# Three unused buffers that shift the split sums of g within SBUF

## The chip, the cores and the metric

The kernel runs on one core of a Trainium2 chip. The metric is the device time of one execution in microseconds (us), lower is better. A core has a matrix engine (PE, with its weight loads shown apart as PEld), a vector engine (DVE), a scalar engine (ACT), GpSimd (POOL), and SyncE (SP), which here only issues transfers. They share an on-chip memory, SBUF, of 128 partitions; an address below is a byte offset that holds in every partition. "Modulo 256" is that offset's remainder.

## The reference

For four batches of 768 tokens and eight heads of 64, a retention layer runs over the tokens, and a feed-forward layer follows:

```python
state = gamma * state + outer(k[t], v[t])      # per head, t = 0..767
x[t]  = q[t] @ state / sqrt(64)                # 3072 tokens x 512
h = x @ w_in                                   # 512 -> 2048
g = h * clip(h + 3, 0, 6) / 6
out = g @ w_out                                # 2048 -> 512
```

All is float32.

## The kernel before

The feed-forward products are made from float32 numbers that are split into a high and a low part (`high` on ACT, line 219; `low` on DVE, line 222), each of a 32-bit matmul type; a product is three matmuls: high by high, high by low, low by high.

**First stage.** The retention, the conversion of the weights, and h run together. h comes in 96 tiles of 128 features by 512 tokens, twelve matmuls each (line 505). ACT (line 512) and DVE (line 516) turn a tile into g, in one of three buffers `g` of 2,048 bytes, and an ACT-issued transfer writes it to the DRAM tensors `gd` (line 539). The order on PE, DVE, ACT and SP is the order of the code here. The first stage ends with the h tiles of the last token unit; from there only PE keeps the order of the code (`order`), while a scheduler sets the order of the other engines by its own estimates of when inputs are ready.

**Second stage.** out = g @ w_out is made in a scheme of seven block products in place of eight (ids 1 to 7). The tokens are taken in three blocks `sb` of 1,024. Each block has four groups, `GROUPS = ((4, 5), (1, 6), (7,), (2, 3))`, and each group goes over four chunks `c` of the features. For a chunk, two transfers bring g back from `gd` into a buffer `gv`; DVE adds or subtracts its halves (lines 136 and 139) into a kept sum `spare` (or in place); then each operand (`gv`, the sum, or both) is split into a buffer `gc` of 8,192 bytes, ACT writing the high half and DVE the low half; and PE makes twelve matmuls of 512 columns from each `gc` (line 782), with the weights `w` standing and `gc` streaming. Results gather in PSUM (`o`), are scaled and combined into `kept_p`, `kept_q`, `kept_v` and `spare` by ACT and DVE (lines 723, 726, 139), and SP stores them to `out` (line 730). The very last product is cut in pieces, and the last store is issued by ACT.

There are 84 operands, and they go round five `gc` buffers: number n takes buffer n modulo 5. Buffers 0 and 1 (tags `gc0`, `gc1`) lie in the pool `late`; buffers 2, 3 and 4 have one pool each, `left["gc0"]`, `left["gc1"]`, `left["gc2"]`:

```python
i = n_gc % 5
pool = late if i < 2 else left[f"gc{i - 2}"]
```

So seventeen operands use each of buffers 0 to 3, and sixteen use buffer 4. The pools `left` stand one behind the other in the order gv0, gv1, gc2, v, p, gc0, gc1, q, on memory that the first stage used for its conversions, for x and for the three `g` buffers. A tile placed there waits for the last users of the bytes it covers.

Every tile that PE reads in this kernel begins at 0 modulo 256. Some smaller constants do not: `mask` lies at 1568 and `cmask` at 2848, both 32 modulo 256.

Of the kernel before, what the change touches and what calls it, by code (L numbers as in the profile page):

```python
# [9 lines left out]
F32 = mybir.dt.float32  # L10
# [10 lines left out]
P = 128  # L21
# [10 lines left out]
def retention_ffn(ctx: ExitStack, tc: tile.TileContext, qkv, w_in, w_out, dvs, dkc, dqc, dmc, tab, out, B, H, S, D):  # L32
# [59 lines left out]
    edge = ctx.enter_context(tc.tile_pool(name="edge", bufs=1, side="right"))  # L92
# [35 lines left out]
    def nm(s):  # L128
        return f"{s}_{next(serial)}"
# [551 lines left out]
    for u, jj in steps[STEADY:]:  # L681
# [8 lines left out]
    left = {  # L690
        n: ctx.enter_context(tc.tile_pool(name=f"left_{n}", bufs=1, reuse_waits="tile"))
        for n in ("gv0", "gv1", "gc2", "v", "p", "gc0", "gc1", "q")
    }
    ends = ctx.enter_context(ExitStack())
    ps_o = [
        ends.enter_context(tc.tile_pool(name=f"ps_o{i}", bufs=1, space=PSUM, reuse_waits="tile", side=side))
# [215 lines left out]
```

## Time and profile before

| | |
|---|---|
| Median of 3 runs | 572.21 us (571.96 to 573.33) |
| The profiled execution | 572.05 us |
| Its span, first to last instruction | 570.3 us |
| PE, DVE, ACT busy | 99%, 75%, 44% of the span |
| Second stage on PE | 1,008 matmuls from 338.06 us on |
| Granted PE clock | 1.00 throughout |

Busy time is a share of the span. A PE that is called busy may still be paced by something, so the pace (time from one matmul's start to the next) is read from how many matmuls lie in a stretch. The profile's rows name tiles without their buffer numbers; `gc<-gv` and `gc<-spare` are the two kinds of split, and both halves of both kinds are 1,024 elements per partition.

### The profile page before, as it was taken

To read this page: it belongs to the slowest core of one execution; us is meant where nothing else is said; L and a number is where in the kernel's file an instruction comes from. 1 tells how busy PE (TensorE), PEld (TensorE's weight loads), DVE (VectorE), ACT (ScalarE), POOL (GpSimd) and SP (SyncE) were. 2 spreads that over 40 slices of the span, in tenths; PEclk is the share of its full clock that TensorE was granted. 3 is DMA by queue.
4 is the path that set the end of the run, shared out by engine and by line. 5 is a ranking of instruction groups with operands and counts; after the bars stand their busy time and mean duration, and the time that the engine had idled before them with its cause. 6 is when DMAs were issued, how large, how long until landed. Compare 5 with 4: busy or idle time off the path is not lost.

```text
span 570.3 us, 11862 instructions
## 1 busy us (share of the span) xinstructions
PE 563.5 (99%) x4832; PEld 462.6 (81%) x4832; DVE 429.6 (75%) x594; ACT 249.2 (44%) x388; POOL 44.2 (8%) x50
## 2 busy tenths in 40 slices
PE   8999999999999999999999999999999999999997
PEld 6777888888888888888888888888888888888885
DVE  5879879942777678887737989679776698676881
ACT  4863434532444443444434654444335443344430
POOL 3001110220111111122000000000000000000000
PEclk9999999999999999999999999999999999999999
DMA  8946787762656666667543485565744747636611
GB/s 314 369 140 220 232 278 228 259 227 92 220 206 223 216 223 215 231 231 260 165 161 115 150 292 189 175 226 167 263 165 132 240 162 258 206 115 189 213 75 74
DMA packets 60626, 115.68 MB, mean 203 GB/s; under 512 B 6166, under 2 KB 6934, under 8 KB 60572
## 3 DMA queue, kind: packets, MB, share of 16 engines
q1 hardware_dynamic: 46304, 89.54, 47.8%
q10 hardware_dynamic: 14268, 25.39, 11.7%
q8 instruction: 38, 0.62, 0.5%
q14 instruction: 16, 0.13, 0.1%
HBM read 83.45 MB, written 31.46 MB: 201 GB/s over the span
## 4 chain that ended last, share of the span: by engine, by line
PE 94%; DVE 3%; DMA 1%; ACT 0%; issue 0%; SPq 0%; DVEq 0%
PE h L505 45%; PE o L782 40%; PE uz L458 3%; PE y L458 3%; PE sc L458 2%; DMA early<-in_qkv 1%; DMA st<-in_w_in 1%; DVE we L200 1%; DVE x L222 0%; DVE am L381 0%; DVE w L222 0%; DVE g L516 0%; DVE wb L187 0%; DVE xr L609 0%; DVE wb L195 0%
## 5 line engine op out<-in xcount | busy, mean ns | idle before, releaser
L505 PE MATMUL h<-x,w 128*128 128x512 f32 x1152 | 270.1, 393 | 0.2
L505 PEld LDWEIGHTS h<-x,w 128*128 128x128 f32 x1152 | 213.9, 188 | 46.4 <-DVE w L222 0.6
L782 PE MATMUL o<-gc,w 128*128 128x512 f32 x1008 | 228.6, 389 | 0.0
L782 PEld LDWEIGHTS o<-gc,w 128*128 128x128 f32 x1008 | 189.2, 188 | 39.3
L512 ACT ACTIVATE g<-h,three 128x512 f32<-128x512 f32 x96 | 65.8, 687 | 109.7 <-PE h L505 81.1
L516 DVE SCALAR_TENSOR_TENSOR g<-g,h 128x512 f32<-128x512 f32 x96 | 65.5, 684 | 56.2 <-ACT g L512 56.0
L219 ACT ACTIVATE gc<-gv 128x1024 fp32r<-128x1024 f32 x48 | 50.9, 1060 | 61.0 <-PE o L782 55.2
L222 DVE TENSOR_TENSOR gc<-gv,gc 128x1024 fp32r<-128x1024 f32 x48 | 58.7, 1222 | 22.5 <-ACT gc L219 22.5
L219 ACT ACTIVATE gc<-spare 128x1024 fp32r<-128x1024 f32 x36 | 38.2, 1061 | 50.3 <-PE o L782 43.3
L222 DVE TENSOR_TENSOR gc<-spare,gc 128x1024 fp32r<-128x1024 f32 x36 | 44.0, 1221 | 10.1 <-ACT gc L219 10.0
L192 ACT ACTIVATE we<-we,ebias 128x512 int32<-128x512 int32 x32 | 23.0, 719 | 17.1 <-DVE we L183 16.3
L219 ACT ACTIVATE w<-ww 128x384 fp32r<-128x384 f32 (+2 forms) x34 | 18.6, 552 | 24.9 <-DVE ww L206 20.6
L200 DVE SCALAR_TENSOR_TENSOR we<-st,we 128x512 int32<-128x512 int32 x32 | 23.0, 720 | 2.3 <-ACT we L192 2.2
L195 DVE SCALAR_TENSOR_TENSOR wb<-st,wb 128x512 f32<-128x512 uint32 x32 | 23.0, 720 | 0.7
L347 POOL TENSOR_TENSOR qs<-qt,dq 128x512 f32<-128x512 f32 x16 | 23.0, 1439 | 6.3 <-DMA dq<-in_decays_q 6.3
L206 DVE SCALAR_TENSOR_TENSOR ww<-wb,we 128x512 f32<-128x512 f32 x32 | 22.9, 715 | 0.8
L462 ACT ACTIVATE state<-uz 128x256 f32<-128x256 f32 x39 | 14.8, 379 | 19.5 <-PE y L458 9.7
L222 DVE TENSOR_TENSOR w<-ww,w 128x384 fp32r<-128x384 f32 (+2 forms) x34 | 20.4, 604 | 1.5 <-ACT w L219 1.4
L136 DVE TENSOR_TENSOR spare<-spare,gv 128x1024 f32<-128x1024 f32 x12 | 14.7, 1223 | 6.1 <-DMA gv<-gd 6.0
L343 POOL TENSOR_TENSOR kn<-kn,ccst 128x512 f32<-128x512 f32 x8 | 9.0, 1128 | 120.9 <-DMA kn<-in_qkv 85.0
L458 PE MATMUL y<-qs,state 64*64 64x64 f32 x480 | 18.3, 222 | 0.0
L458 PE MATMUL y<-am,vn 64*64 64x64 f32 x512 | 18.1, 219 | 0.0
(69 smaller groups left out, 417.9 us busy)
## 6 DMA issues: line engine op xcount, KB each, us to landing
gd<-g ACTq DMA_DIRECT2D x96, 256.0 KB, 2.9
gv<-gd SPq DMA_DIRECT2D x48, 512.0 KB, 4.7
gv<-gd SPq DMA_DIRECT2D x48, 256.0 KB, 3.0
st<-in_w_in SPq DMA_DIRECT2D x32, 256.0 KB, 3.9
st<-in_w_out SPq DMA_DIRECT2D x16, 512.0 KB, 5.8
early<-in_qkv SPq DMA_DIRECT2D x28, 256.0 KB, 4.6
kt<-in_qkv SPq DMA_DIRECT2D x16, 256.0 KB, 3.5
qt<-in_qkv SPq DMA_DIRECT2D x16, 256.0 KB, 3.9
```

The source lines that it names most:

```text
L192: nc.scalar.activation(out=t["e"], in_=t["e"], func=AF.Relu, scale=8.0, bias=ebias)
L195: nc.vector.scalar_tensor_tensor(out=t["b"].bitcast(F32), in0=lo.bitcast(U32), scalar=2.0**-32, in1=t["b"], op0=ALU.mult, op1=ALU.add)
L200: nc.vector.scalar_tensor_tensor(out=t["e"], in0=hi, scalar=-2147483648, in1=t["e"], op0=ALU.bitwise_and, op1=ALU.bitwise_or)
L206: nc.vector.scalar_tensor_tensor(out=t["w"], in0=t["b"].bitcast(F32), scalar=2.0**-20, in1=t["e"].bitcast(F32), op0=ALU.mult, op1=ALU.mult)
L219: nc.scalar.activation(out=hi, in_=src, func=AF.Copy)
L222: nc.vector.tensor_tensor(out=lo, in0=src, in1=hi, op=ALU.subtract)
L347: nc.gpsimd.tensor_tensor(out=t["qs"], in0=t["qt"], in1=d, op=ALU.mult)
L458: nc.tensor.matmul(out_, lhs, rhs, start=start, stop=True, skip_group_check=True)
L505: nc.tensor.matmul(h, t[:, o, a], xs[u][b][:, k], start=k + n == 0, stop=(k, n) == (NK - 1, 2), skip_group_check=True)
L512: return g, nc.scalar.activation(out=g, in_=h, func=AF.Relu, bias=three).ins
L516: ins = nc.vector.scalar_tensor_tensor(out=g, in0=g, scalar=6.0, in1=h, op0=ALU.min, op1=ALU.mult)
L782: nc.tensor.matmul(acc[i][h] if last else acc[i][:, h], w2c[j][:, RIGHT[i], x, h], gc[:, y, jj], start=j == 0 and n == 0, stop=j == NFP - ...
```

## The change

```diff
     left = {
         n: ctx.enter_context(tc.tile_pool(name=f"left_{n}", bufs=1, reuse_waits="tile"))
         for n in ("gv0", "gv1", "gc2", "v", "p", "gc0", "gc1", "q")
     }
+    for n, edge in (("gc2", 64), ("gc0", 128), ("gc1", 96)):
+        left[n].tile([P, edge // 4], F32, tag="edge", name=nm("edge"))
```

Three buffers are allocated that no instruction touches. They push what stands behind them upwards:

| Tile | Address before | Address after | After, modulo 256 |
|---|---|---|---|
| gc buffer 4 (`gc2`) | 163840 | 163904 | 64 |
| kept_v | 172032 | 172096 | 64 |
| kept_p | 176128 | 176192 | 64 |
| gc buffer 2 (`gc0`) | 180224 | 180416 | 192 |
| gc buffer 3 (`gc1`) | 188416 | 188704 | 32 |
| kept_q | 196608 | 196896 | 32 |

All of these lay at 0 modulo 256. gc buffers 0 and 1, all `gv`, `spare` and all weights stay where they were. Buffer 3 ended at 196608, where the first of the three `g` buffers begins; now it ends at 196896, so it covers the first 288 bytes of that buffer.

No instruction is added or removed, but the scheduler places some differently at the seam between the stages. The three new buffers take three serial numbers, so a name's last number is three higher after the change: what is gc_4239 before is gc_4242 after. It is the fourth operand, the sum of chunk 1, in buffer 3. gc_4236 (after: gc_4239) is the third operand; gc_4270 and gc_4273 (after: gc_4273 and gc_4276) are the fifth and sixth, from chunk 2.

ACT at the seam, high halves, before:

```order
L219 ACTIVATE gc_4236<-gv_4232 128x1024 [waits DMAHW3_49,DMAHW1_49]
L539 DMA gd_74<-g_4151 128x512 [waits DVE_49]
L219 ACTIVATE gc_4239<-spare_4191 128x1024 [waits DVE_49]
L219 ACTIVATE gc_4270<-gv_4266 128x1024 [waits DMAHW6_49,DMAHW5_49,Activation_49]
L219 ACTIVATE gc_4273<-spare_4192 128x1024 [waits DVE_49,PE_49,Activation_49]
L219 ACTIVATE gc_4304<-gv_4300 128x1024 [waits DMAHW0_49,DMAHW2_49,PE_49,Activation_49]
```

ACT at the same place after:

```order
L219 ACTIVATE gc_4239<-gv_4235 128x1024 [waits DMAHW3_49,DMAHW1_49]
L539 DMA gd_74<-g_4151 128x512 [waits DVE_49]
L219 ACTIVATE gc_4273<-gv_4269 128x1024 [waits DMAHW6_49,DMAHW5_49,Activation_49]
L219 ACTIVATE gc_4276<-spare_4195 128x1024 [waits DVE_49,PE_49,Activation_49]
L219 ACTIVATE gc_4242<-spare_4194 128x1024 [waits DMAHW4_49]
L219 ACTIVATE gc_4307<-gv_4303 128x1024 [waits DMAHW0_49,DMAHW2_49,PE_49,Activation_49]
```

The fourth operand's high half has moved behind the two of chunk 2, and it waits for a transfer: the one that writes out the last g tile of the first `g` buffer (g_4097), which ACT issues right behind the relu of the next h tile.

DVE at the seam, sums and low halves, before:

```order
L139 TENSOR_TENSOR spare_4191<-gv_4232 128x1024 [waits DMAHW3_49,DMAHW1_49]
L222 TENSOR_TENSOR gc_4236<-gv_4232,gc_4236 128x1024 [waits Activation_49]
L139 TENSOR_TENSOR spare_4192<-gv_4266 128x1024 [waits DMAHW6_49,DMAHW5_49,PE_49]
L222 TENSOR_TENSOR gc_4239<-spare_4191,gc_4239 128x1024 [waits Activation_49]
L222 TENSOR_TENSOR gc_4270<-gv_4266,gc_4270 128x1024 [waits Activation_49]
L222 TENSOR_TENSOR gc_4273<-spare_4192,gc_4273 128x1024 [waits Activation_49]
L139 TENSOR_TENSOR spare_4192<-gv_4300 128x1024 [waits DMAHW2_49,DMAHW0_49]
```

and after:

```order
L139 TENSOR_TENSOR spare_4194<-gv_4235 128x1024 [waits DMAHW3_49,DMAHW1_49]
L222 TENSOR_TENSOR gc_4239<-gv_4235,gc_4239 128x1024 [waits Activation_49]
L139 TENSOR_TENSOR spare_4195<-gv_4269 128x1024 [waits DMAHW6_49,DMAHW5_49,PE_49]
L222 TENSOR_TENSOR gc_4273<-gv_4269,gc_4273 128x1024 [waits Activation_49]
L222 TENSOR_TENSOR gc_4276<-spare_4195,gc_4276 128x1024 [waits Activation_49]
L222 TENSOR_TENSOR gc_4242<-spare_4194,gc_4242 128x1024 [waits DMAHW4_49,Activation_49]
L139 TENSOR_TENSOR spare_4195<-gv_4303 128x1024 [waits DMAHW2_49,DMAHW0_49]
```

Here too the fourth operand's low half has moved behind those of the fifth and the sixth.

PE uses the operands in the unchanged order. Around the fourth operand it now reads:

```order
L784 MATMUL o_4199<-gc_4239,w_353_2955 128x512 x3
L784 MATMUL o_4200<-gc_4242,w_312_2629 128x512 [waits Activation_49]
L784 MATMUL o_4200<-gc_4242,w_312_2629 128x512 [waits DVE_49]
L784 MATMUL o_4200<-gc_4242,w_312_2629 128x512
L784 MATMUL o_4200<-gc_4242,w_353_2955 128x512 x3
L784 MATMUL o_4200<-gc_4242,w_312_2629 128x512 x3
L784 MATMUL o_4200<-gc_4242,w_353_2955 128x512 x3
L784 MATMUL o_4199<-gc_4273,w_396_3300 128x512 x3
```

The first matmul of an operand waits for ACT (the high half), the second for DVE (the low half). What moved is which engine step is the last one that PE waits for there; the fifth operand, which had such waits of its own, has none left, since the fourth is now made behind it.

## The prediction

> **What bounds the kernel now.** The first view is the page: its busy shares and its chain of work that ended last.
>
> ```profile
> PE 563.5 (99%) x4832; PEld 462.6 (81%) x4832; DVE 429.6 (75%) x594; ACT 249.2 (44%) x388; POOL 44.2 (8%) x50
> PE 94%; DVE 3%; DMA 1%; ACT 0%; issue 0%; SPq 0%; DVEq 0%
> ```
>
> PE carries 94% of the chain. The chain in order of time (columns: start, length, what) says how its second stage runs, which is the only stage with moved tiles.
>
> ```profile
> 289.03 49.19 PE h L505 x216
> 338.22 228.49 PE o L782 x1008
> 566.73 0.42 DVE kept_v L726
> 567.16 0.33 DVEq L908
> ```
>
> The 1,008 matmuls of the second stage stand on the chain as one unbroken piece: 228.49 us / 1,008 = 226.7 ns each. So nothing that ACT, DVE or a transfer does there reaches the end of the program today, and there are just two ways in which the change can: the pace of a matmul changes, or a first wait appears in this piece.
>
> Is the pace steady? The third view counts work by stretches of the second stage (length, then busy time and count of each engine, the clock, the transfers' share and rate).
>
> ```profile
> 358.00:396.00 38.00, 38.00 (x169) 31.48 (x168) 30.35 (x26) 17.47 (x18) 0.00 (x0) 1.00 0.61 194
> 396.00:434.00 38.00, 38.00 (x170) 31.45 (x169) 29.44 (x26) 14.84 (x15) 0.00 (x0) 1.00 0.58 194
> 434.00:472.00 38.00, 38.00 (x169) 31.47 (x168) 30.24 (x26) 17.59 (x18) 0.00 (x0) 1.00 0.61 194
> 472.00:510.00 38.00, 38.00 (x169) 31.47 (x168) 29.51 (x26) 14.84 (x15) 0.00 (x0) 1.00 0.59 194
> 510.00:548.00 38.00, 38.00 (x170) 31.45 (x169) 29.89 (x26) 17.59 (x18) 0.00 (x0) 1.00 0.52 166
> ```
>
> Every stretch of 38 us has 169 or 170 matmuls, the one or two at its edges counted in, at a clock of 1.00. DVE is busy 29.4 to 30.4 us of it, ACT 14.8 to 17.6. The groups show what the two do with the gc tiles, and the waits who is ahead of whom.
>
> ```profile
> L222 DVE TENSOR_TENSOR gc<-gv,gc 128x1024 fp32r<-128x1024 f32 x48 | 58.7, 1222 | 22.5 <-ACT gc L219 22.5
> L219 ACT ACTIVATE gc<-gv 128x1024 fp32r<-128x1024 f32 x48 | 50.9, 1060 | 61.0 <-PE o L782 55.2 <-DVE gc L222 3.3 <-DMA gv<-gd 2.5
> ...
> ACT gc L219 <- PE o L782: 98.6, 62, 1.7
> ```
>
> ACT stands still 98.6 us in all, in 62 waits, because PE still reads the buffer that ACT wants: the makers of operands are ahead of PE and are throttled by it.
>
> **The change part by part.** *Nothing is computed less or more.* Five gc buffers remain five, so the distance by which the makers may run ahead is the same.
>
> *The pace of PE on moved buffers.* Buffers 2, 3 and 4 hold 17 + 17 + 16 = 50 of 84 operands, so 50 x 12 = 600 of the 1,008 matmuls stream from an address that is no longer 0 modulo 256. No matmul of this trace does that, so the cost is bounded from both sides. Upwards: 512 float32 columns are 2,048 bytes, eight pieces of 256 bytes from an aligned start and nine from another; if the pace went with the pieces, each matmul would cost 226.7 / 8 = 28.3 ns more, 17.0 us in all. Downwards: the quickest 512-column stream of the trace is that of the small bf16 tables.
>
> ```profile
> 6.01 0.82 PE L559 MATMUL t<-bits 6*128 6x512 bf16 x3
> ...
> L559 PE MATMUL t<-bits x6: 371/379/384, 6.0 to 17.2; 6*128 6x512 bf16 x6
> ```
>
> Three of them take 0.82 us, the last one's own 0.379 included, so their pace is (0.82 - 0.379) / 2 = 0.2205 us, 6.2 ns under that of the second stage; 600 x 6.2 = 3.7 us is the most that a better address could give. Between +17.0 and -3.7 us I take zero, by the nearest rows that do read SBUF off 0 modulo 256: DVE's products with `mask` and `cmask` (both 32 modulo 256), beside its product with `early` (0 modulo 256).
>
> ```profile
> L381 DVE TENSOR_TENSOR am<-sc,mask 128x512 f32<-128x512 f32 x12 | 7.9, 684 | 3.8 <-issue 3.6
> L426 DVE TENSOR_TENSOR am<-sc,cmask 128x512 f32<-128x512 f32 x16 | 11.0, 688 | 6.2 <-PE y L458 6.2
> L609 DVE TENSOR_TENSOR xr<-y,early 128x512 f32<-128x512 f32 x8 | 5.5, 686 | 4.3 <-PE y L458 4.3
> ```
>
> 684 and 688 ns off the boundary, 686 ns on it: the address shows no price on DVE. For ACT's and DVE's writes into the moved buffers I take zero as well, by the same rows, and the cover is large. PE uses one operand in 12 x 0.2267 = 2.72 us, so 14 in 38 us, of which 14 x 50 / 84 = 8.3 are moved; DVE has 38 - 30.35 = 7.65 us free in its fullest stretch. Each moved low half could take 7.65 / 8.3 = 0.92 us more than today before PE would wait. A gain there would be worth nothing.
>
> The stores of kept_p, kept_v and kept_q now read from 64 and 32 modulo 256. All but the last are far behind PE. Of that one the row is
>
> ```profile
> out<-kept_v ACTq DMA_DIRECT2D x1, 128.0 KB, 1.7
> ```
>
> and I take no change for it. [...]
>
> *The seam.* The fourth operand is now split behind the fifth and sixth. This is the only place where PE may wait. The time line of DVE and ACT there before (start, length, then the step; DVE: sum and low half of the third and so on, as listed with the change):
>
> ```profile
> 338.06 9.23 PE L782 MATMUL o<-gc,w 128*128 128x512 f32 x40
> ...
> 338.84 1.05 ACT L219 ACTIVATE gc<-gv 128x1024 fp32r<-128x1024 f32 x1
> ...
> 339.58 1.22 DVE L139 TENSOR_TENSOR spare<-gv 128x1024 f32<-128x1024 f32 x1
> ...
> 340.72 1.22 DVE L222 TENSOR_TENSOR gc<-gv,gc 128x1024 fp32r<-128x1024 f32 x1
> 340.84 1.06 ACT L219 ACTIVATE gc<-spare 128x1024 fp32r<-128x1024 f32 x1 [0.94 <-DVE spare L139]
> 341.80 1.04 ACT L219 ACTIVATE gc<-gv 128x1024 fp32r<-128x1024 f32 x1
> 341.85 1.22 DVE L139 TENSOR_TENSOR spare<-gv 128x1024 f32<-128x1024 f32 x1
> ...
> 342.99 1.22 DVE L222 TENSOR_TENSOR gc<-spare,gc 128x1024 fp32r<-128x1024 f32 x1
> 343.19 1.06 ACT L219 ACTIVATE gc<-spare 128x1024 fp32r<-128x1024 f32 x1 [0.34 <-DVE spare L139]
> 344.12 1.22 DVE L222 TENSOR_TENSOR gc<-gv,gc 128x1024 fp32r<-128x1024 f32 x1
> ```
>
> Two habits are read from it: steps of DVE follow each other at 1.135 us (340.72, 341.85, 342.99, 344.12), those of ACT at 0.96 (340.84, 341.80); and a result is used 0.04 to 0.12 us after its end (the sum ending at 340.80, ACT at 340.84; the sum ending at 343.07, ACT at 343.19). PE reaches the fourth operand's second matmul, which needs its low half, at 338.06 + 37 x 0.2267 = 346.45. Before, that half ended at 342.99 + 1.22 = 344.21, 2.2 us early. Now:
>
> - ACT makes the fifth operand's high half behind the third's, long before DVE asks for it at 342.99.
> - The sixth needs the sum of chunk 2, which ends at 343.07: ACT from 343.11 or 343.19, until 344.17 or 344.25. DVE starts its low half 0.04 later, 344.21 to 344.29, a little behind the 344.12 at which it is free.
> - The fourth's high half goes 0.96 behind the sixth's and ends by 345.21, before PE's first use at 346.22. Its low half starts 1.135 us behind the sixth's, 345.35 to 345.42, ends 1.22 later, 346.57 to 346.64, and reaches PE at about 346.61 to 346.68.
>
> PE waits 0.16 to 0.23 us there; I take **0.2 us**, with 0.1 and 0.4 as ends, since a handover can take 0.04 or 0.12 more. Queued behind that wait is all the rest of PE's stage, so it goes to the end in full. The new wait for the transfer costs nothing: ACT issues it at 335.54, and the slowest of the 96 lands in 6.7 us,
>
> ```profile
> 335.54 0.33 ACTq L539 DMA_DIRECT2D gd<-g  x1
> ...
> DMA to landing us min/median/max: 2.0/2.9/6.7
> ```
>
> at 342.24, 1.8 us before ACT comes to that step. What is late next is DVE by some 0.15 us at the low half of the seventh operand (chunk 3), which PE needs only at 338.06 + 73 x 0.2267 = 354.6.
>
> **The sum.** The profiled execution took 572.05 us with a span of 570.3; +0.2 gives a span of 570.5 and 572.25 us. The runs' median is 572.21, 0.16 above that execution, so the forecast for a median is 572.4 us.
>
> **The rivals.**
>
> *PE reads a moved buffer more slowly (slower).* Place: the 600 matmuls; price: up to 28.3 ns each, 589 us; if only a finer piece of 64 bytes counts, buffer 3 alone pays, 17 x 12 = 204 matmuls x 226.7 / 32 = 7.1 ns, 1.4 us, 573.8. It decides from (1.72 - 0.2) / 600 = 2.5 ns a matmul. For it: no matmul of this trace has ever read off the boundary, so nothing excludes it. Against it: the DVE rows above. [...] No run so far shows a matmul that could tell.
>
> *DVE or ACT writes a moved buffer more slowly (slower).* Only past 0.92 us for each low half. Twice today's 1.135 would make 8.3 x 1.135 - 7.65 = 1.8 us of waiting in 38 us, some 10.7 us over the 228 of the stage: 583 us. The even cost in the rows above speaks against it.
>
> *Streams collide today (faster).* All tiles start at the same remainder; if PE lost time to ACT's and DVE's writes at the same position, spreading the buffers would give up to 3.7 us, 568.7 us. Against it: DVE's and ACT's steps drift against PE's (1.135 and 0.96 against 0.2267 us), so their positions meet in every way, yet no stretch is slower than another, and the last of them, with a lighter transfer load of 166 GB/s, is none the faster.
>
> *The seam costs more.* If the transfer landed at 346 rather than 342.2, PE would wait 2 us: 574.4. Its landing is bounded by 96 others, so this is a part of the slow tail.
>
> **How the numbers follow.** A measurement of this kernel tells about 0.3%, 1.7 us, from no change. The forecast, an unchanged pace with 0.2 us at the seam, has 0.71, and its own range is 571.7 to 573.4. A slower PE has 0.12, slower ACT or DVE 0.04, a longer seam 0.03: slower 0.19 together. Collisions that vanish have 0.10. The range goes from 570.4, half-way into the gain, to 576.0, past the finer piece and the longer seam.
>
> **What would show it.** Right: an L782 row of 1,008 matmuls with the same pace in every stretch (169 or 170 in 38 us), and one idle time of PE near 346.4 us, 0.1 to 0.4 us long, ended by DVE's gc step. Wrong: 38-us stretches with fewer than 168 matmuls, or waits of PE on L219 or L222 beyond the seam, or gc steps on ACT or DVE off 1,060 and 1,222 ns. The forecast falls if the pace differs between matmuls from buffers 0 and 1 and the rest.

## The result

| | Before | Changed |
|---|---|---|
| Median | 572.22 us (571.96 to 573.33, 4 runs) | 576.24 us (576.07 to 576.42, 4 runs) |
| Span of the profiled execution | 570.3 us | 574.3 us |

The changed kernel is slower: 1.0067 of the time before, with a 95% interval of 1.0049 to 1.0084. The prediction was wrong: it said 572.4 us and no measurable change, and the measured time lies 0.24 us past the upper end of its range. One of the ten runs of the first experiment below took 1,443 us, and the ratio there is formed without it.

The page after the change looks almost the same. The chain of work in order of time (start, length, what) shows where the 4 us lie; its last pieces are these.

```profile
289.08 49.19 PE h L505 x216
338.27 8.47 PE o L784 x37
346.75 223.95 PE o L784 x971
570.73 0.42 DVE kept_v L728
571.15 0.33 DVEq L910
```

The first stage ends where it ended (338.27 against 338.22), and the 216 h matmuls before it take 49.19 us as before. The one piece of 1,008 matmuls is now two, 37 and 971: that is the forecast wait at the seam. But the 971 behind it take 223.95 us, 230.6 ns each, where 226.7 was forecast. The stretches of 38 us (length, busy time and count of each engine, clock, transfers) say the same:

```profile
358.00:396.00 38.00, 38.00 (x167) 30.89 (x166) 29.46 (x26) 17.43 (x17) 0.00 (x0) 1.00 0.60 193
396.00:434.00 38.00, 38.00 (x167) 30.92 (x166) 29.16 (x26) 14.87 (x14) 0.00 (x0) 1.00 0.58 194
434.00:472.00 38.00, 38.00 (x167) 30.96 (x166) 29.14 (x26) 17.30 (x17) 0.00 (x0) 1.00 0.57 180
472.00:510.00 38.00, 38.00 (x167) 30.99 (x166) 29.60 (x26) 14.26 (x15) 0.00 (x0) 1.00 0.62 209
510.00:548.00 38.00, 38.00 (x167) 30.89 (x166) 29.12 (x25) 17.45 (x17) 0.00 (x0) 1.00 0.52 166
```

167 matmuls in each, where there were 169 or 170, at a clock of 1.00, and PE called busy throughout. A slower pace hides in a "busy" engine: no idle time appears in any of these stretches. The groups (moved and unmoved buffers together) show that ACT and DVE take no longer for their splits, and are still ahead:

```profile
L222 DVE TENSOR_TENSOR gc<-gv,gc 128x1024 fp32r<-128x1024 f32 x48 | 58.6, 1221 | 24.7 <-ACT gc L219 24.6
L219 ACT ACTIVATE gc<-gv 128x1024 fp32r<-128x1024 f32 x48 | 50.9, 1060 | 63.1 <-PE o L784 51.5 <-DVE gc L222 6.8 <-ACT gc L219 2.7
...
ACT gc L219 <- PE o L784: 89.1, 53, 1.8
```

The 1,008 matmuls are used in a known order, twelve to an operand, and operand n lies in buffer n modulo 5. So the starts of the matmuls in the trace can be sorted by buffer: the time from an operand's first matmul to the next operand's first, divided by twelve, averaged over the operands of a buffer (the fourth operand, with the wait at the seam, and the last left out). All paces by buffer below are made in this way.

| gc buffer | 0 | 1 | 2 | 3 | 4 |
|---|---|---|---|---|---|
| before: begins at, modulo 256 | 0 | 0 | 0 | 0 | 0 |
| pace, ns | 226.7 | 226.7 | 226.7 | 226.7 | 226.7 |
| changed: begins at, modulo 256 | 0 | 0 | 192 | 32 | 64 |
| pace, ns | 228.6 | 226.7 | 233.3 | 233.1 | 229.8 |

Each moved buffer has its own pace, the same in the second and the third block of tokens, and within 0.4 ns of that in the first. Buffer 0, which did not move but follows buffer 4, is slow in the first five of its twelve matmuls each time that it does, and then back at 226.7. Over 226.7 this makes 17 x 12 x 6.7 = 1.4 us in buffer 2, 17 x 12 x 6.4 = 1.3 in buffer 3, 16 x 12 x 3.1 = 0.6 in buffer 4, 17 x 12 x 2.0 = 0.4 in buffer 0: 3.7 us together. At the seam two spacings (from one matmul's start to the next) of 399 and 339 ns stand in place of 227: 0.28 us. With the 0.05 us by which the stage begins later these are the 4.0 us of the span.

### The profile page after: what moved, and what is told of

The parts are those of the page before. It is cut to its first block, busy times and chain, and to the rows that moved or that the text cites. A ratio compares the mean times of both kernels' runs of the same rounds, so it can differ in the third digit from the quotient of the medians.

```text
span 574.3 us, 11862 instructions
## 1 busy us (share of the span) xinstructions
PE 567.6 (99%) x4832; PEld 462.6 (81%) x4832; DVE 424.7 (74%) x594; ACT 249.1 (43%) x388; POOL 45.7 (8%) x50
## 4 chain that ended last, share of the span: by engine, by line
PE 95%; DVE 2%; DMA 2%; issue 0%; SPq 0%; ACT 0%; DVEq 0%
PE h L505 47%; PE o L784 40%; PE uz L458 3%; PE y L458 3%; PE sc L458 2%; DMA st<-in_w_in 1%; DMA early<-in_qkv 1%; DVE am L381 0%; DVE x L222 0%; DVE xr L609 0%; DVE we L200 0%; SPq L157 0%; DVE ww L206 0%; ACT w L219 0%; DVE w L222 0%
## 5 line engine op out<-in xcount | busy, mean ns | idle before, releaser
L784 PE MATMUL o<-gc,w 128*128 128x512 f32 x1008 | 232.6, 392 | 0.0
L219 ACT ACTIVATE gc<-gv 128x1024 fp32r<-128x1024 f32 x48 | 50.9, 1060 | 63.1 <-PE o L784 51.5
L222 DVE TENSOR_TENSOR gc<-gv,gc 128x1024 fp32r<-128x1024 f32 x48 | 58.6, 1221 | 24.7 <-ACT gc L219 24.6
L222 DVE TENSOR_TENSOR gc<-spare,gc 128x1024 fp32r<-128x1024 f32 x36 | 43.9, 1221 | 11.4 <-ACT gc L219 11.1
L343 POOL TENSOR_TENSOR kn<-kn,ccst 128x512 f32<-128x512 f32 x8 | 10.7, 1335 | 122.0 <-DMA kn<-in_qkv 111.1
L136 DVE TENSOR_TENSOR spare<-spare,gv 128x1024 f32<-128x1024 f32 x12 | 14.7, 1221 | 6.1 <-DMA gv<-gd 6.1
```

Source lines behind the costliest of these rows:

```text
L219: nc.scalar.activation(out=hi, in_=src, func=AF.Copy)
L222: nc.vector.tensor_tensor(out=lo, in0=src, in1=hi, op=ALU.subtract)
L784: nc.tensor.matmul(acc[i][h] if last else acc[i][:, h], w2c[j][:, RIGHT[i], x, h], gc[:, y, jj], start=j == 0 and n == 0, stop=j == NFP - ...
```

## The experiments

### The seam alone: all three buffers moved, but by multiples of 256

```diff
-    for n, edge in (("gc2", 64), ("gc0", 128), ("gc1", 96)):
+    for n, edge in (("gc2", 256), ("gc0", 256), ("gc1", 256)):
```

> The three unused buffers have 256 bytes each, so the three gc buffers stand at other places than before, but again at 0 modulo 256; every engine has the same instructions in the same order as in the changed kernel, the seam included. Theory A (what a matmul streams from an address off 0 modulo 256 is slower): 1,008 matmuls at 226.7 ns, one wait of PE of 0.2 to 0.3 us at the seam, 572.4 us. Theory B (the seam's other order, and the engines' other phase after it, cost the 4 us): 576.2 us, as the changed kernel. Theory C (the place in SBUF, not its remainder): about 576.

Measured: 572.58 us beside 572.16 for the kernel before, a ratio of 1.0008 (0.9998 to 1.0018). The three buffers have moved by 256, 512 and 768 bytes, and all five stream at 226.7 ns. The stretches of 38 us, and the wait of PE's weight loads at the seam:

```profile
358.00:396.00 38.00, 38.00 (x169) 31.49 (x168) 30.43 (x27) 17.55 (x17) 0.00 (x0) 1.00 0.60 193
396.00:434.00 38.00, 38.00 (x169) 31.45 (x169) 29.73 (x26) 14.87 (x14) 0.00 (x0) 1.00 0.58 194
434.00:472.00 38.00, 38.00 (x170) 31.45 (x169) 29.86 (x27) 17.64 (x17) 0.00 (x0) 1.00 0.61 194
...
PEld o L784 <- DVE gc L222: 0.5, 1, 0.5
```

169 or 170 matmuls are back. So neither the seam nor the place in SBUF costs the 4 us (theories B and C fall), and the remainder does (theory A stands). The seam is worth some 0.4 us here: two spacings of 482 and 337 ns in the trace. The measured times cannot tell that from zero.

### Other remainders

```diff
-    for n, edge in (("gc2", 64), ("gc0", 128), ("gc1", 96)):
+    for n, edge in (("gc2", 128), ("gc0", 96), ("gc1", 192)):
```

> Buffers 4, 2 and 3 begin at 128, 224 and 160 modulo 256; all instructions and their order as in the changed kernel. Theory A with 'off 256' alone as the condition: all three buffers stream at 229 to 233 ns, 576 us. Theory A with pieces of 128 bytes: buffer 4 at 226.7 ns, the others at about 233, 575 us. Theory A with pieces of 64 bytes: buffer 4 at 226.7, buffers 2 and 3 (32 modulo 64) at 233. Theory B: as the changed kernel whatever the addresses, 576.2 us, with the same pace in each buffer as there.

Measured: 576.69 us in one run. Buffer 4 (128) streams at 232.8 ns, buffer 2 (224) at 233.5, buffer 3 (160) at 233.8. "Off 256" alone is the condition: a buffer that is aligned to 128 bytes pays too, so no smaller piece explains it.

### The same remainders in other buffers

```diff
-    for n, edge in (("gc2", 64), ("gc0", 128), ("gc1", 96)):
+    for n, edge in (("gc2", 192), ("gc0", 96), ("gc1", 32)):
```

> The changed kernel's three remainders in other buffers: buffer 4 at 192, buffer 2 at 32, buffer 3 at 64; instructions and order as in the changed kernel. Theory A: the pace goes with the remainder, so buffer 4 streams at 233 ns, buffer 2 at 233, buffer 3 at 229 to 230; 576 us. If the pace goes with the buffer (its neighbours in time, its place): buffer 2 at 233, 3 at 233, 4 at 229.8 as in the changed kernel.

Measured: 576.09 us in one run. Buffer 4 (now 192): 232.5 ns; buffer 2 (now 32): 233.6; buffer 3 (now 64): 229.9. The pace goes with the remainder and not with the buffer.

### No sums or splits beside PE

The second and third block reuse what lies in the five buffers:

```diff
+                if sb == 0:
+                    with ExitStack() as first:
...
+                else:
+                    ops = []
+                    for _ in ids:
+                        ops.append(ring[-5:][(n_gc - len(ring)) % 5])
+                        n_gc += 1
```

> The changed kernel's addresses, but the second and third block of 1,024 tokens read no g back, make no sums and no splits: their matmuls stream whatever the five gc buffers hold from the first block (so the output of these tokens is not the reference's). PE then has 672 of its 1,008 matmuls without writes of ACT and DVE to gc beside them. Theory A (address alone): the pace in these blocks stays 233, 233 and 229.8 ns in buffers 2, 3 and 4, the stage at some 232 us, 576 us. Theory D (the streams of ACT or DVE collide with PE's since the buffers no longer stand at one remainder): 226.7 ns in these blocks, 672 x 3.9 ns = 2.6 us less than the changed kernel, 573.6 us.

Measured: 576.56 us in one run. In three stretches, one for each block (the columns as above: PE, PEld, DVE, ACT, POOL, clock, transfers' share and rate), first the changed kernel:

```profile
338.00:416.00 78.00, 78.00 (x340) 63.25 (x339) 63.85 (x56) 34.99 (x35) 0.00 (x0) 1.00 0.64 211
416.00:492.00 76.00, 76.00 (x332) 61.86 (x331) 59.00 (x51) 32.43 (x31) 0.00 (x0) 1.00 0.58 190
492.00:568.00 76.00, 76.00 (x332) 61.90 (x331) 51.81 (x46) 28.22 (x27) 0.00 (x0) 1.00 0.42 136
```

and this experiment:

```profile
338.00:416.00 78.00, 77.99 (x339) 63.30 (x338) 55.42 (x48) 30.70 (x30) 0.00 (x0) 1.00 0.45 152
416.00:492.00 76.00, 76.00 (x331) 61.84 (x331) 8.36 (x7) 3.08 (x3) 0.00 (x0) 1.00 0.07 26
492.00:568.00 76.00, 76.00 (x332) 61.91 (x331) 8.07 (x8) 3.08 (x3) 0.00 (x0) 1.00 0.08 28
```

DVE's work falls from 59.00 to 8.36 us, ACT's from 32.43 to 3.08, the transfers from 190 to 26 GB/s, and PE makes 331 or 332 matmuls all the same. The paces by buffer in these blocks are 228.8, 226.7, 233.3, 233.1 and 229.8 ns, those of the changed kernel. Buffer 1, which begins at 0, has 226.7 ns with this company and without. So the price does not need the other engines' splits or the transfers for them (theory D falls). What is left besides the streamed operand is the standing one, the weights in their SBUF tiles: 1,008 weight loads of 188 ns stand beside the 1,008 matmuls here.

### Weights, x and three buffers together at 64

From the kernel before:

```diff
-    const.tile([P, 40], F32, name="edge")
+    const.tile([P, 56], F32, name="edge")
```

> From the kernel before, with one unused constant buffer 64 bytes longer: weights, x, gv and spare, and gc buffers 2, 3 and 4 all begin at 64 modulo 256, and gc buffers 0 and 1, on the other side of SBUF, stay at 0. The engines' instructions and their order are those of the kernel before. Theory E (only the remainder of the streaming operand counts): buffers 0 and 1 at 226.7 ns, buffers 2 to 4 at 229.0 as buffer 4 of the changed kernel, 600 x 2.3 = 1.4 us, and the 1,152 h matmuls with x at 64 too, 2.7 us: 576.3 us. Theory F (the distance between the streaming and the standing operand counts, modulo 256): buffers 2 to 4 and the h stage at 226.7, since both operands stand at 64; buffers 0 and 1, 192 behind the weights, at 233: 408 x 6.6 = 2.7 us, 574.9 us. Theory G (either operand off 0 costs): everything at 229 or more, 577 or more.

Measured: 575.02 us beside 572.15, a ratio of 1.0051 (1.0036 to 1.0066). The chain's pieces:

```profile
288.69 49.19 PE h L505 x216
337.88 231.55 PE o L782 x1008
```

The h stage keeps its 49.19 us for 216 although x and the weights begin at 64. In the second stage the buffers that did **not** move, 0 and 1, stream at 233.3 ns, and buffers 3 and 4, at 64 like the weights, at 226.7; buffer 2, which follows buffer 1, has 228.3, with four of its first five matmuls slow. That is theory F: what counts is the distance between the two operands, the streamed one's remainder less the weights'. Buffers 0 and 1 stand at 0 - 64 = 192, and have the pace that 192 had in the changed kernel.

### The weights alone at 64

From the kernel before, the weights' pool 64 bytes up and what lies behind it back to 0:

```diff
-    const.tile([P, 40], F32, name="edge")
+    const.tile([P, 56], F32, name="edge")
...
     wpool = ctx.enter_context(tc.tile_pool(name="wpool", bufs=NSLOT))
+    pad = ctx.enter_context(tc.tile_pool(name="pad", bufs=1))
...
+    pad.tile([P, 48], F32, name="pad")
```

> From the kernel before: only the weights' pool (with spare and one of the six x tiles) moved to 64 modulo 256, all gc buffers, gv and the other x tiles at 0 modulo 256. Order of all engines as before. Theory E (streaming operand alone): every o matmul at 226.7 ns, 572.2 us. Theory F (distance of the two operands, here 192 everywhere but in one x): 1,008 o matmuls and some 960 h matmuls at 233, 13 us: 585 us. Theory G: between, 575 to 577 us.

Measured: 584.39 us beside 572.15, a ratio of 1.0215 (1.0198 to 1.0232). No gc buffer has moved off 0, and yet:

```profile
292.98 50.59 PE h L508 x216
343.57 235.21 PE o L785 x1008
...
358.00:396.00 38.00, 38.00 (x165) 30.61 (x164) 29.10 (x26) 17.25 (x17) 0.00 (x0) 1.00 0.56 180
396.00:434.00 38.00, 38.00 (x165) 30.61 (x164) 30.10 (x26) 14.60 (x14) 0.00 (x0) 1.00 0.60 202
```

235.21 / 1,008 = 233.3 ns in every buffer, and 50.59 / 216 = 234.2 in the h stage, where it was 227.7. Theory E (the streamed operand alone) said 572.2 us, theory F 585. With this the cause is settled as far as an address goes: the distance modulo 256 between what a matmul streams and what stands. Here the distance is 0 - 64 = 192 for every `gc` buffer, and the pace is the one that 192 had in the changed kernel, 233.3 ns.

### All three buffers at 64

```diff
-    for n, edge in (("gc2", 64), ("gc0", 128), ("gc1", 96)):
+    for n, edge in (("gc2", 64), ("gc0", 256), ("gc1", 256)):
```

> From the changed kernel, instructions and order as there: buffers 2, 3 and 4 all begin at 64 modulo 256. Theories E and F alike: the three stream at 229 to 229.8 ns as buffer 4 did there, 600 x 2.7 = 1.6 us, with some 0.4 us in the first matmuls of buffer 0 and 0.4 us at the seam 574.6 us. If what counts is a difference between neighbours in time: less than that, 226.7 ns inside the run of 36 matmuls and extra time only at its ends, 573 us.

Measured: 575.29 us in one run, 0.7 over the forecast. In the run of 36 matmuls at 64, buffer 2 has 230.3 ns, buffers 3 and 4 have 228.9; buffer 0, behind them, 230.4, nine of its first ten matmuls slow. So a distance of 64 costs 2.2 ns in the middle of a run, and entering or leaving it costs more. The slow matmuls behind such a buffer are no sign of their own addresses, for the kernel before has the same ones with everything at 0. Where its h matmuls start anew at 288.96 us, the spacings behind the first are 230, 236, 229, 232 and 231 ns, and then 227; in the changed kernel's buffer 0 they are 231, 236, 228, 233 and 231. So they show a stream that comes back to its pace after a disturbance. How many matmuls that takes is not explained: five in those two places, ten in buffer 0 here (one of them quicker than 226.7), and ten where h starts anew at 275.80 us in the kernel before.

### Smaller distances, and a search for a better one

```diff
-        return pool.tile([P, 2, CP, UT], F32R, tag=f"gc{i}", name=nm("gc"))
+        skip = {2: 4, 3: 60, 4: 24}.get(i)
+        if skip is None:
+            return pool.tile([P, 2, CP, UT], F32R, tag=f"gc{i}", name=nm("gc"))
+        t = pool.tile([P, 2 * CP * UT + 64], F32R, tag=f"gc{i}", name=nm("gc"))
+        return t[:, skip : skip + 2 * CP * UT].rearrange("p (a j n) -> p a j n", a=2, j=CP)
```

> Weights and gc buffers 0 and 1 at 0 modulo 256; buffers 4, 2 and 3 begin 96, 16 and 240 bytes past a multiple of 256, by a wider buffer of which the matmuls and splits use a part that begins so far in; order of all engines as in the changed kernel. Theory F (any distance between the two operands that is no multiple of 256 costs): all three at 229 to 234 ns, 576 us. If pieces of 32 bytes hide a distance of 16: buffer 2 at 226.7. If some distance is better than 0: a buffer under 226.7 ns, and then a kernel with all buffers at that distance beats both, by up to the 6.2 ns that the quickest stream of the trace leaves.

Measured: 576.58 us in one run; buffer 4 (96) at 232.8 ns, buffer 2 (16) at 231.5, buffer 3 (240) at 236.2. Even 16 bytes cost. All distances together, each with the pace of the buffer that had it (entering included, except the 228.9, which is the middle of a run):

| Distance modulo 256 | 0 | 16 | 32 | 64 | 96 | 128 | 160 | 192 | 224 | 240 |
|---|---|---|---|---|---|---|---|---|---|---|
| Pace, ns | 226.7 | 231.5 | 233.1 to 233.6 | 228.9 to 230.3 | 232.8 | 232.8 | 233.8 | 232.5 to 233.3 | 233.5 | 236.2 |

None is under 226.7, so there is no better placement among them than that of the kernel before, and no version here beats both.

### Half the weight load

To see whether the weight load takes part, all matmuls of the second stage but the first into each result load 64 weight columns in place of 128, once at the changed kernel's addresses and once, as in the first experiment, at distance 0:

```diff
+                                cols = slice(0, P if j == 0 and n == 0 else P // 2)
                                 nc.tensor.matmul(
-                                    acc[i][h] if last else acc[i][:, h],
-                                    w2c[j][:, RIGHT[i], x, h],
+                                    acc[i][h][cols] if last else acc[i][cols, h],
+                                    w2c[j][:, RIGHT[i], x, h, cols],
```

> The changed kernel's addresses and order, but all matmuls of the second stage except the first into each result load only 64 of their 128 weight columns (so half of the output rows miss most of their sum). The streamed operand stays 512 columns. Beside the same at distance 0 (the run e10): theory H (the price belongs to the weight load that reads SBUF while the last matmul still streams, and goes with what it reads): half the extra of the changed kernel, buffer 2 at 3.3 ns over e10, buffer 3 at 3.2, the stage 1.8 us over e10's. Theory I (the price belongs to the streaming alone): the whole extra, 6.7 and 6.4 ns, the stage 3.7 us over e10's.

> The same halved weight loads with every gc buffer at 0 modulo 256 (the three moved by 256 bytes as in the first experiment). All matmuls at one pace: 226.7 ns if the fixed part of the pace over the 512 columns does not come from the weight load, down to about 220 if it does (the 0.2205 us of the small bf16 tables, whose weight loads take 92 ns in place of 188). 572.5 us or down to some 566.

Measured: 575.88 us off 0 and 575.46 at 0, one run each. The chain's piece and the weight loads' group off 0,

```profile
337.93 232.60 PE o L785 x1008
...
L785 PEld LDWEIGHTS o<-gc,w 128*64 128x64 f32 (+1 forms) x1008 | 137.6, 137 | 94.9 <-DVE gc L222 0.4
```

and at 0:

```profile
338.23 231.91 PE o L785 x1008
...
L785 PEld LDWEIGHTS o<-gc,w 128*64 128x64 f32 (+1 forms) x1008 | 137.4, 136 | 94.5 <-DVE gc L222 0.5
```

Both expectations missed. Weight loads of half the columns, 136 ns against 188, made the matmuls at distance 0 *slower*: 231.91 / 1,008 = 230.1 ns with the wait at the seam in it, 229.8 to 229.9 by buffer, against 226.7. And of the price of the addresses little is left: 232.60 - 231.91 = 0.7 us for the stage, where theory H said 1.8 and theory I 3.7; by buffer, 232.1 against 229.9 ns in buffer 2, 230.9 against 229.8 in buffer 3, 229.6 against 229.9 in buffer 4. The streamed operand and its addresses are the same and the price is not, so it is not the streaming's alone (theory I falls). Halving the weight columns also halves the rows of the result that a matmul writes, so these two runs do not show which of the two changes the pace. Theory H has the direction, but not the size, and it did not foresee the loss at distance 0. The single spacings say what that loss looks like: with full weight loads at distance 0 they are 226 or 227 ns each, while here they go round in 229, 224, 227, 234, 230, 236 through most of the stage. Why is open.

## Why the prediction was wrong

**The step that failed** is "Between +17.0 and -3.7 us I take zero", the pace of PE on moved buffers. It measured 3.7 us: 3.3 in the three moved buffers, and 0.4 in buffer 0 behind them, where the prediction had no term. The bounds held, the value between them was wrong, and the reason given for it was a row of another engine: DVE's products with `mask` at 32 modulo 256 (684 ns, against 686 at 0) say how DVE reads SBUF. That reading was right for DVE and ACT, whose splits kept 1,221 and 1,060 ns in the changed kernel. For PE no row spoke, and with no row near it, zero should not have had 0.71.

**The rival with the right place** was "PE reads a moved buffer more slowly", with a chance of 0.12. The prediction's signs of being wrong ("38-us stretches with fewer than 168 matmuls", "the pace differs between matmuls from buffers 0 and 1 and the rest") are just what was seen. Its two prices were not: nine pieces for eight would cost 28.3 ns a matmul, and 64-byte pieces 7.1 ns in buffer 3 alone; measured were 3 to 7 ns in all three. And its mechanism was incomplete, since a buffer at 64 streams at 226.7 ns when the weights stand at 64 too. Moving the weights alone by 64 bytes slowed the 1,008 matmuls from 226.7 to 233.3 ns each.

**Streams collide today** was rightly kept small: with the splits and their transfers taken away the pace did not change, in buffer 1 at 0 (226.7 ns) no more than in the moved ones (233.3, 233.1 and 229.8).

**The seam** was right, a little small. The forecast was 0.2 us between 0.1 and 0.4; the trace has 0.28. The time line of the changed kernel:

```profile
343.04 1.22 DVE L222 TENSOR_TENSOR gc<-gv,gc 128x1024 fp32r<-128x1024 f32 x1
343.24 2.01 ACT L219 ACTIVATE gc<-spare 128x1024 fp32r<-128x1024 f32 x2 [1.97 <-DVE spare L139]
344.33 2.36 DVE L222 TENSOR_TENSOR gc<-spare,gc 128x1024 fp32r<-128x1024 f32 x2
...
346.75 0.76 PEld L784 LDWEIGHTS o<-gc,w 128*128 128x128 f32 x4 [0.44 <-DVE gc L222]
```

ACT makes the high halves of the sixth and the fourth operand one behind the other until 345.25, DVE the low halves until 344.33 + 2.36 = 346.69 (forecast: 346.57 to 346.64), and PE goes on at 346.75, where it could have at 338.11 + 37 x 0.2267 = 346.50 at the pace of before. Two errors partly cancel in the 0.28: the slow buffer 2 brought PE to the seam 0.08 us later than forecast, and the matmul behind the wait took 0.11 us over the pace, which the forecast left out. In the first experiment, where PE keeps the forecast pace, the seam cost 0.37 us, near the upper end of 0.4. The transfer that the fourth operand now waits for cost nothing, as forecast: ACT goes from the sixth operand to the fourth without idle time.

**The last store** landed in 1.8 us in place of 1.7. The rows of `kept_v`, first before and then changed:

```profile
out<-kept_v SPq DMA_DIRECT2D x2, 512.0 KB, 2.7
out<-kept_v ACTq DMA_DIRECT2D x1, 128.0 KB, 1.7
...
out<-kept_v SPq DMA_DIRECT2D x2, 512.0 KB, 2.9
out<-kept_v ACTq DMA_DIRECT2D x1, 128.0 KB, 1.8
```

The traces of all runs together tell this from the spread. The last store took 1,715 to 1,730 ns in the five runs in which `kept_v` begins at 0 modulo 256, and 1,742 to 1,753 ns in the seven in which it begins at 64, 128 or 192. So taking no change for it was wrong by some 0.03 us. The cost is no higher for 128 or 192 than for 64. The 512 KB row went from 2.7 us in those five runs to 2.8 or 2.9 in the seven, far behind PE, where it costs nothing.

**What stays open** is the mechanism. Shown are the condition (the distance modulo 256 between streamed and standing operand), that the splits and the transfers for them are not needed for it, and that halving the weight columns changes the price (0.7 us for the stage in place of 3.7). No run shows why both addresses count, and neither the loss at distance 0 with half the weights (229.8 to 229.9 ns against 226.7) nor the order of the paces (64 the cheapest at 228.9 ns, 240 the dearest at 236.2) is derived from the condition.

## What to carry to other kernels

Where matmuls run back to back as here, with new weights for each stream of 512 float32 columns, place the tiles that PE streams and the tiles it takes as weights at the same remainder modulo 256 bytes, and check the pace as matmuls per fixed stretch: a PE that is 99% busy can still lose 3% to addresses (235.21 us for the second stage against 228.49, with the weights alone at 64), with no wait to show it. Other shapes and types of matmul were not tried. An unused buffer, a longer constant or another pool order in front of either of the two can shift all that stands behind it, so a change that adds a small tile should be read by addresses as well. And a price that no row of the engine in question shows is not zero because another engine's row is even.

## What was not expected of the hardware

- The pace of a 128x128 by 512 float32-split matmul was 226.7 ns at a distance of 0 modulo 256 and 228.9 to 236.2 ns at every other distance tried, down to 16 bytes.
- It went with the distance and not with either address: both at 64 ran at 226.7, one at 0 and one at 64 at 228.9 or 233.3, by which of the two was ahead.
- A disturbed stream of matmuls took five to ten of them to come back to 226.7 ns, nearly all of these 1 to 13 ns slow: in a buffer at distance 0 behind one at another distance, and just so at distance 0 where a stream starts anew.
- Weight loads of 64 columns, 136 ns in place of 188, made matmuls at distance 0 slower, 229.8 to 229.9 against 226.7 ns by buffer.
- A store of 128 KB from SBUF took 1,742 to 1,753 ns from a start at 64, 128 or 192 modulo 256 and 1,715 to 1,730 from 0, with no more for 128 or 192 than for 64.
